# GpSimd takes two steps of the weight preparation in a fused attention and FFN kernel on one core, with the order of the work set anew

## The chip, the cores and the metric

The kernel runs on one core of one Trainium2 chip. The metric is device time in microseconds (us) of one execution. Before the change the median of three runs is 1265.73 us (1262.9 to 1267.84).

## The reference, cut to what matters

Eight batches of eight heads attend over 576 positions with head size 64; only scores within `tau` of the row's maximum count. The heads' outputs, side by side, go through an FFN whose activation is a ratio of polynomials.

```python
scores = scale * (q @ k.T)
thresh = scores.max(-1) - tau
attn = softmax(where(scores >= thresh, scores, -1e9))
x = (attn @ v) as [8*576, 512]
h = x @ w_in                      # 512 -> 2048
g = (a0 + a1*h + a2*h**2 + a3*h**3) / (1 + |b0|*|h| + |b1|*h**2 + 1e-6)
out = g @ w_out                   # 2048 -> 512
```

## The kernel before, in words

**Attention.** The heads of a batch are taken in four pairs; a unit is one block of 128 queries of a pair (`unit_ops`, L767), and the last 64 rows of both heads make a half unit. TensorE forms the scores (L810, for half units L800), VectorE takes their maximum (L818), ScalarE thresholds and exponentiates (L833, L837), and ScalarE and VectorE split the result into a high and a low fp16 part (L347, L859), which DMA transposes on SyncE's queue turn around (L869). For the first batch `f_diag` and `f_tr` (L875, L882, L887) transpose on TensorE instead and `f_avp` (L912) multiplies by V; later `f_av` (L928) does. The result is split again into `x` (L938, L944).

**FFN.** `moe_ops` takes 256 positions and four of the sixteen groups of 128 hidden columns at a time: first layer (L1045), scale (L1054), the rational function on ScalarE and VectorE (L1059 to L1087), split into `g` (L339, L1095), second layer (L1104).

**Weights.** Both weight matrices arrive as 64-bit words, each word the bits of a double. `decode_ops` (L483) turns a tile of 128x512 of them into fp32, for 16 tiles of `w_in` and 16 of `w_out`. `ld` issues the transfer on GpSimd's queue; `f1` (L506, ScalarE) takes the high words; `f2` (L509, ScalarE) scales the low words by 2^-29; `f4` (L513, VectorE) shifts; `f6` (L354, VectorE) adds both. For `w_out`, `f_wh` rounds to the 'wh' part (L341 or L339) and `f_wl` (L593, VectorE) forms the remainder. Each is needed before the first FFN block that uses its group. A wait keeps transfers apart: a tiny GpSimd instruction (L498) reads the third last tile when that was issued within the last 9 us.

**V.** `load_v_ops` (L680) clears two corners of a V tile (L690), loads it (L696, L700) on GpSimd's queue, and takes its maximum (`mx`, L711 or L709). After a batch's fourth maximum `scale_ops` (L427) makes the batch's scale: two VectorE steps (L437, L442), one matmul (`f_all`, L446), more VectorE steps. Four V tiles exist, so a load waits until the attention that used the tile has multiplied by it.

**Order.** Nothing is ordered by the engines at run time. Every step is recorded with `op(engine, duration, key, function, ...)`, and `Plan.order` (L193) lists them: it keeps a clock for each engine, lets the ready step with the lowest key start, and picks the engine of a step that may run on two. `TURN` and `KIND` are tables added to the keys, `EARLY` and `PRICE` weigh ScalarE against VectorE. 'GD' is GpSimd's queue, whose steps before were transfers only. Where the plan sees TensorE idle in its first 400 us, it puts filler matmuls (`f_warm`, L1248) into 0.6 of the gap; the fillers compute nothing that is used.

Of the kernel before, what the change touches and what calls it, by code (L numbers as in the profile page):

```python
# [80 lines left out]
EARLY = {"ACT": 1.6309, "DVE": 3.9296}  # L81
EARLY_END = 714.5248
PRICE = {"ACT": 0.9171, "DVE": 2.3360}

TURN = [
# [22 lines left out]
KIND = [  # L108
# [8 lines left out]
BEGIN = 1.4  # L117
WIRE, LATER = 1.25, 0.3
# [22 lines left out]
class Plan:  # L141
# [3 lines left out]
    LAT = {"PE": 0.27, "ACT": 0.28, "DVE": 0.22, "POOL": 0.16, "DMA": 2.3, "GD": 2.7}  # L145
    OWN = {"PE": 0.0, "ACT": 0.15, "DVE": 0.13, "POOL": 0.1, "DMA": 2.3, "GD": 2.7}
# [15 lines left out]
    def op(self, eng, dur, key, fn, after=(), take=(), drop=(), wire=None):  # L162
        engs = {eng: dur} if isinstance(eng, str) else eng
        o = Op(engs, key, fn, [x for x in after if x is not None], list(take), list(drop))
        o.wire = wire and (wire[0] * WIRE, wire[1] + LATER)
        o.turn, o.kind = self.turn, self.kinds.setdefault(fn.__code__, len(self.kinds))
        turn = TURN[o.turn] / 1000 if o.turn < len(TURN) else 0.0
        o.key += turn
        o.key += KIND[o.kind] / 1000 if o.kind < len(KIND) else 0.0
        o.rank = self.rank + turn  # L170
        self.ops.append(o)
        return o
# [20 lines left out]
    def order(self):  # L193
# [19 lines left out]
        left, wire = len(self.ops), 0.0  # L213
        while left:
# [28 lines left out]
            o.eng, o.dur = e, o.engs[e]  # L243
            for x in o.engs:
# [53 lines left out]
def masked_attention_rational_ffn(  # L298
# [28 lines left out]
    for name, n in [*POOLS.items(), ("q", NQ), ("k", NQ), ("v", NV)]:  # L327
        plan.pool(name, n)
# [962 lines left out]
```

## Time and profile before

| what | value |
|---|---|
| median of the runs, us | 1265.73 |
| profiled execution: time, us | 1266.8 |
| profiled execution: span, first to last instruction, us | 1265.0 |
| TensorE matmul busy | 1226.9 us, 97% |
| VectorE busy | 1188.0 us, 94% |
| ScalarE busy | 1118.3 us, 88% |
| GpSimd busy | 97.8 us, 8% |
| TensorE's mean granted clock, share of full | 0.991 |

The 1.8 us between time and span lie outside the profiled instructions. The busy shares are averages over stages with different limits: weights are prepared in the first 160 us, attention and FFN run side by side until 1140 us, and only FFN is left after it.

### The profile page before, as it was taken

How to read it: one execution, taken by the hardware profiler on the slowest of the kernel's cores; microseconds unless marked ns; L12 is line 12 of the kernel's file. 1: busy time of each engine (PE TensorE's matmuls, PEld its weight loads, DVE VectorE, ACT ScalarE, POOL GpSimd, SP SyncE). 2: the span in 40 equal slices, each digit the busy share in tenths (PEclk: the TensorE clock that was granted, in tenths of full speed). 3: DMA queues.
4: the chain of work that ended last, by engine and by line, in shares of the span. 5: the costliest groups of instructions: out<-in, count | busy, mean ns of one | idle time of the engine just before them, and what ended most of it. 6: DMA issues, size and time to landing. Idle time of an engine off the chain costs nothing. (4 is left out here: it accounts for less than half of the span.)

```text
span 1265.0 us, 25738 instructions
## 1 busy us (share of the span) xinstructions
PE 1226.9 (97%) x9650; PEld 961.6 (76%) x9650; DVE 1188.0 (94%) x1830; ACT 1118.3 (88%) x2185; POOL 97.8 (8%) x217
## 2 busy tenths in 40 slices
PE   8899999999999999999999999999999989999998
PEld 6677777777777777767777777777777767778886
DVE  6999899999999999999999899999999979998787
ACT  7999999999989899988898999899999979895564
POOL 4110000010001100101001100021001100000000
PEclk9999999999999999999999999999999989999999
DMA  6454644675556654665664666667456664542000
GB/s 193 136 167 129 149 81 85 134 151 119 114 95 146 126 110 102 124 121 89 124 116 80 131 125 96 122 120 139 90 112 125 132 109 88 116 88 45 18 17 17
DMA packets 338603, 138.54 MB, mean 110 GB/s; under 512 B 312624, under 2 KB 321712, under 8 KB 338480
## 3 DMA queue, kind: packets, MB, share of 16 engines
q1 hardware_dynamic: 326656, 103.40, 43.9%
q0 software_dynamic: 11072, 32.91, 8.9%
q8 instruction: 76, 1.25, 0.4%
q10 hardware_dynamic: 752, 0.59, 0.2%
q14 instruction: 47, 0.39, 0.1%
HBM read 52.17 MB, written 9.44 MB: 49 GB/s over the span
## 5 line engine op out<-in xcount | busy, mean ns | idle before, releaser
L1104 PE MATMUL banks<-wp,g 128*128 128x512 f32 x1728 | 449.1, 408 | 3.2 <-DVE g L1095 1.7
L1104 PEld LDWEIGHTS banks<-wp,g 128*128 128x128 f32 x1728 | 317.1, 191 | 82.6 <-DVE g L1095 4.4
L1045 PEld LDWEIGHTS <-wi 128*128 128x128 f16 x3456 | 328.8, 98 | 65.3 <-issue 23.3
L1045 PE MATMUL banks<-x,wi 128*128 128x256 f16 x3072 | 360.4, 274 | 3.8 <-ACT t L1054 3.3
L837 ACT ACTIVATE e<-e,cf 128x576 f32<-128x576 f32 x288 | 222.3, 779 | 0.2
L859 DVE SCALAR_TENSOR_TENSOR e<-e,st,hi 128x576 f16<-128x576 f32 x252 | 204.3, 811 | 7.2 <-ACT hi L347 6.5
L833 ACT ACTIVATE e<-banks,st 128x576 f32<-128x576 f32 x288 | 207.2, 739 | 4.2 <-DMA pT<-e 1.9
L347 ACT ACTIVATE hi<-e,st 128x576 f16<-128x576 f32 x225 | 171.0, 770 | 30.2 <-DVE st L848 25.3
L810 PE MATMUL banks<-KK,QQ 64*128 64x64 f32 (+1 forms) x1024 | 175.5, 455 | 7.4 <-ACT e L833 4.5
L818 DVE TENSOR_REDUCE st<-banks 128x2 f32<-128x1152 f32 x128 | 172.3, 1346 | 8.0 <-PE banks L810 7.2
L810 PEld LDWEIGHTS banks<-KK,QQ 64*128 64x128 f32 x1024 | 115.1, 188 | 77.0 <-issue 46.9
L1054 ACT ACTIVATE t<-banks,hsc 128x512 f32<-128x512 f32 (+1 forms) x192 | 106.6, 577 | 26.0 <-PE banks L1045 16.4
L928 PE MATMUL banks<-pT,V 128*64 128x256 f16 (+1 forms) x2520 | 121.7, 250 | 2.6 <-DVE xr L944 2.4
L928 PEld LDWEIGHTS <-V 128*64 128x64 f16 x2520 | 103.7, 111 | 23.3 <-issue 18.8
L1081 DVE SCALAR_TENSOR_TENSOR t<-t,co,t 128x1024 f32<-128x1024 f32 (+1 forms) x73 | 92.2, 1263 | 18.7 <-ACT t L1075 18.6
L1072 ACT ACTIVATE t<-t,co 128x1024 f32<-128x1024 f32 (+1 forms) x73 | 82.9, 1136 | 28.3 <-DVE t L1078 27.0
L1095 DVE TENSOR_TENSOR g<-t,g 128x512 fp32r<-128x512 f32 x144 | 95.2, 683 | 0.8 <-ACT g L339 0.7
L1087 DVE SCALAR_TENSOR_TENSOR t<-t,co,t 128x1024 f32<-128x1024 f32 (+1 forms) x73 | 92.2, 1264 | 0.6
L1065 DVE SCALAR_TENSOR_TENSOR t<-t,co 128x1024 f32<-128x1024 f32 (+1 forms) x73 | 92.2, 1263 | 0.3 <-ACT t L1054 0.3
L1068 DVE SCALAR_TENSOR_TENSOR t<-t,co 128x1024 f32<-128x1024 f32 (+1 forms) x73 | 92.2, 1263 | 0.0
L1078 DVE SCALAR_TENSOR_TENSOR t<-t,co,t 128x1024 f32<-128x1024 f32 (+1 forms) x73 | 92.2, 1263 | 0.0
L1084 DVE SCALAR_TENSOR_TENSOR t<-t,t 128x1024 f32<-128x1024 f32 (+1 forms) x73 | 87.9, 1204 | 0.5
(116 smaller groups left out, 1183.5 us busy)
## 6 DMA issues: line engine op xcount, KB each, us to landing
KK<-in_kT_dram SPq DMA_DIRECT2D x108, 144.0 KB, 3.0
t<-in_w_in_dram POOLq DMA_DIRECT2D x16, 512.0 KB, 4.9
t<-in_w_out_dram POOLq DMA_DIRECT2D x16, 512.0 KB, 4.8
V<-in_v_dram POOLq DMA_DIRECT2D x28, 256.0 KB, 4.4
out_dram<-u POOLq DMA_DIRECT2D x26, 256.0 KB, 3.0
QQ<-in_qT_dram SPq DMA_DIRECT2D x72, 64.0 KB, 2.3
pT<-hi SPq DMA_TRANSPOSE x140, 3.3
pT<-e SPq DMA_TRANSPOSE x140, 3.3
```

Of the source, the lines that this page charges most:

```text
L347: nc.scalar.activation(dst, src, AF.Identity, scale=factor)
L810: mm = nc.tensor.matmul(s[:, d0:d0 + n], QQ[r, t * P:(t + 1) * P], KK[r, k0:k0 + n], **one)
L818: nc.vector.tensor_reduce(box["st"][:, 0:2], box["both"], AX.X, ALU.max, negate=True)
L833: nc.scalar.activation(ev(hh), box["s"][hh], AF.Prelu, scale=SCALE, bias=box["st"][:, 2 + hh:3 + hh], alpha=STEEP)
L837: nc.scalar.activation(e, e, AF.Exp, scale=passes, accum_out=box["st"][:, 4 + hh:5 + hh])
L859: nc.vector.scalar_tensor_tensor(box["lo"][:, c], ev(hh), box["st"][:, 6 + hh:7 + hh], box["hi"][:, c], ALU.mult, ALU.subtract)
L928: nc.tensor.matmul(dst, V[:, c * P + hh * D:c * P + (hh + 1) * D], rhs, start=c == 0 and n == 0, stop=c == NT and n == 2)
L1045: nc.tensor.matmul(d, wi_tile(c, f0 + j, hl), x[:, c, :], start=c == 0 and n == 0, stop=c == NC - 1 and n == 2)
L1054: nc.scalar.activation(box["h3"][:, 2 * k:2 * k + 2, sl], psv[:, :, sl], AF.Identity, scale=hsc[:, b2, g:g + 1])
L1065: nc.vector.scalar_tensor_tensor(box["r"], box["h"], a2, box["h"], ALU.add, ALU.mult)
L1095: nc.vector.tensor_tensor(fr(g[:, 1]), box["r"][:, k * GW:(k + 1) * GW], g[:, 0], ALU.subtract)
L1104: nc.tensor.matmul(acc[tt], fr(g[:, x]), fr(wo[f][y]), start=begins and j == n == 0, stop=ends and j == nb - 1 and n == 2)
```

## The change

The step `f2` goes from ScalarE to GpSimd. The step `f_wl` goes from VectorE to GpSimd. Both are put into the plan's queue 'GD' with the transfers, so that the plan decides where on GpSimd's queue each stands; the tiny waiting instruction L498 goes, and a pool "w" of three takes its place: a weight transfer takes a slot and `f2` gives it back. A matmul of another layout than the one before costs the plan 0.093 us more, and the durations of attention's matmuls are lowered by about two such amounts. The plan expects V's transfers to land later. All order tables are new; only a line of each is shown. Lines of the changed kernel lie 2 to 5 higher in number (L509 is L510, L593 is L595, L446 is L451, L1248 is L1250).

```diff
-EARLY = {"ACT": 1.6309, "DVE": 3.9296}
+EARLY = {"ACT": 1.6376, "DVE": 3.8765}
-PRICE = {"ACT": 0.9171, "DVE": 2.3360}
+PRICE = {"ACT": 0.9166, "DVE": 2.2665}
 TURN = [
-    -22753, -3751, -27085, -7959, -27620, -11402, -9570, -6508, -9214, -7383, -6968, -3656, -3744, -4154, -5879,
+    -22753, -7303, -14653, -13042, -55886, -12787, -11115, 320, -22676, -1808, -1997, -1589, 541, -2218, -1953, 992,
...
+TURNS = 0.093
...
-    LAT = {"PE": 0.27, "ACT": 0.28, "DVE": 0.22, "POOL": 0.16, "DMA": 2.3, "GD": 2.7}
-    OWN = {"PE": 0.0, "ACT": 0.15, "DVE": 0.13, "POOL": 0.1, "DMA": 2.3, "GD": 2.7}
+    LAT = {"PE": 0.27, "ACT": 0.28, "DVE": 0.22, "POOL": 0.16, "DMA": 2.3, "GD": 0.2}
+    OWN = {"PE": 0.0, "ACT": 0.15, "DVE": 0.13, "POOL": 0.1, "DMA": 2.3, "GD": 0.1}
...
+            if e == "PE":
+                o.dur += TURNS if o.mode != mode else 0.0
+                mode = o.mode
...
-            if len(loaded) >= AHEAD and plan.now - loaded[-AHEAD][1] < RECENT:
-                nc.gpsimd.tensor_scalar(cf[0:1, 15:16], loaded[-AHEAD][0][0:1, 0, 1:2].bitcast(F32), 1.0, 1.0, ALU.mult, ALU.mult)
             box["rw"] = load()
-            loaded.append((box["rw"], plan.now))
+            loaded.append(box["rw"])
...
         def f2():
-            nc.scalar.activation(box["rw"][:, :, 0], box["rw"][:, :, 0].bitcast(U32), AF.Copy, scale=2.0 ** -29)
+            nc.gpsimd.tensor_scalar(box["rw"][:, :, 0], box["rw"][:, :, 0].bitcast(U32), 2.0 ** -29, 1.0, ALU.mult, ALU.mult)
...
-        l = op("GD", 2.5, key - 2.0, ld, (), [hold], wire=(1.9, 2.0))
+        wh = Hold("w", 1)
+        l = op("GD", 0.65, key - 2.0, ld, (), [hold, wh], wire=(1.9, 2.3))
...
-        o2 = op("ACT", 0.568, key, f2, [l])
+        o2 = op("GD", 0.87, key, f2, [l], (), [wh])
...
         def f_wl(f=f, box=box):
-            nc.vector.tensor_tensor(fr(wo[f][1]), box["w"], wo[f][0], ALU.subtract)
+            nc.gpsimd.tensor_tensor(fr(wo[f][1]), box["w"], wo[f][0], ALU.subtract)
...
-        wo_done.append(op("DVE", 0.66, key, f_wl, [o], (), [hold]))
+        wo_done.append(op("GD", 1.5, key, f_wl, [o], (), [hold]))
...
-        l = v_loaded[bp] = op(eng, 1.7 if eng == "DMA" else 2.0, max(q, V0 + V1 * pr), ld, (), [vhold], wire=(1.1, 1.5 if eng == "DMA" else 2.5))
+        l = v_loaded[bp] = op(eng, 1.7 if eng == "DMA" else 2.0, max(q, V0 + V1 * pr), ld, (), [vhold], wire=(1.1, 3.0 if eng == "DMA" else 4.5))
...
-        qk = op("PE", 1.36 if full else 1.12, p, f_qk, need, [sh[0]], [kh, qh] * nh)
+        qk = op("PE", 1.175 if full else 0.935, p, f_qk, need, [sh[0]], [kh, qh] * nh, mode=1)
```

The change moves instructions in three places that the prediction speaks of. The first is GpSimd's queue behind the first V loads, where the weights come in; `t` are tiles that hold weights, and `wp` is where the second layer's weights end. Before:

```order
L546 DMA t_68<-in_w_in_dram 128x1024
L546 DMA t_69<-in_w_in_dram 128x1024
L582 DMA t_70<-in_w_out_dram 128x1024
L498 TENSOR_SCALAR cf<-t_68 1x1
L546 DMA t_71<-in_w_in_dram 128x1024
L498 TENSOR_SCALAR cf<-t_69 1x1
L546 DMA t_72<-in_w_in_dram 128x1024
L696 DMA V_157<-in_v_dram 128x4x128
L700 DMA V_157<-in_v_dram 64x64 x2
L546 DMA t_73<-in_w_in_dram 128x1024
```

And now:

```order
L548 DMA t_68<-in_w_in_dram 128x1024
L584 DMA t_69<-in_w_out_dram 128x1024
L548 DMA t_70<-in_w_in_dram 128x1024
L698 DMA V_157<-in_v_dram 128x4x128
L702 DMA V_157<-in_v_dram 64x64 x2
L510 TENSOR_SCALAR t_68<-t_68 128x512
L548 DMA t_71<-in_w_in_dram 128x1024
L510 TENSOR_SCALAR t_69<-t_69 128x512
L548 DMA t_72<-in_w_in_dram 128x1024
L510 TENSOR_SCALAR t_70<-t_70 128x512
L548 DMA t_73<-in_w_in_dram 128x1024
L510 TENSOR_SCALAR t_71<-t_71 128x512
L595 TENSOR_TENSOR wp_1_123<-t_69,wp_0_122 128x512
```

The fourth V load now stands ahead of the fourth weight transfer, and each later transfer stands behind arithmetic on an earlier tile.

The second place is ScalarE's queue in the same stretch, from the second block's exponential on; `u` holds high words, `pT` transposed scores. Before:

```order
L837 ACTIVATE e_78,st_85<-e_78,cf 128x576 x2
L509 ACTIVATE t_68<-t_68 128x512
L509 ACTIVATE t_69<-t_69 128x512
L833 ACTIVATE e_79<-banks,st_86 128x576
L339 COPY pT_82<-banks 128x4x128
L506 ACTIVATE u_76<-t_68 128x512
L339 COPY pT_82<-banks 128x4x128
L339 COPY pT_82<-banks 128x128
L506 ACTIVATE u_74<-t_69 128x512
```

And now:

```order
L507 ACTIVATE u_74<-t_68 128x512
L839 ACTIVATE e_78,st_85<-e_78,cf 128x576 x2
L835 ACTIVATE e_79<-banks,st_86 128x576
L556 ACTIVATE t_68,wm<-t_68 128x512
L344 COPY pT_82<-banks 128x4x128
L835 ACTIVATE e_79<-banks,st_86 128x576
L344 COPY pT_82<-banks 128x4x128
```

The two low-word steps between the exponential and the copies for TensorE's transposes are gone. Over the whole program ScalarE loses all 32 low-word steps and VectorE all 16 remainders; TensorE's fillers go from 81 matmuls to 60, and the number of its changes between scores, attention outputs and the rest from 450 to 449.

The third place is TensorE ahead of a late batch's scale matmul, from the last use of the V tile whose reload that scale waits for. Before, at the last batch (between the rows shown stand 24 first-layer matmuls L1045 and 12 second-layer matmuls L1104):

```order
L928 MATMUL banks<-pT_83,V_156 64x64
...
L1045 MATMUL banks<-x_98,wi 128x256
...
L1104 MATMUL banks<-wp_1_125,g_96 128x512
L810 MATMUL banks<-KK_115,QQ_111 128x64
L810 MATMUL banks<-KK_115,QQ_111 128x512 x2
...
L1104 MATMUL banks<-wp_0_126,g_94 128x512 x2
L1104 MATMUL banks<-wp_1_127,g_94 128x512
L446 MATMUL banks<-u_76,cf 128x128
```

And now, at the last batch but one (between the rows stand 24 L1047, four matmuls of scores, three L1106 and six L1047):

```order
L930 MATMUL banks<-pT_83,V_157 64x64
L812 MATMUL banks<-KK_115,QQ_111 128x64
L812 MATMUL banks<-KK_115,QQ_111 128x512 x2
...
L1047 MATMUL banks<-x_98,wi 128x256
...
L812 MATMUL banks<-KK_114,QQ_110 128x512 x2
...
L1106 MATMUL banks<-wp_1_123,g_95 128x512
...
L1047 MATMUL banks<-x_97,wi 128x256
L451 MATMUL banks<-u_76,cf 128x128
```

At this place the changed order has less work between the two than any batch after the first has in the order before; at the last batch it has more.

## Rows read from the trace of the kernel before

**Rows 1.** The view by stage: the stretch and its length in us, the busy time of PE, PEld, DVE, ACT and POOL with their instructions in brackets, TensorE's granted clock as a share of full, the DMA engines' busy share and GB/s.

```profile
20.00:160.00 140.00, 128.62 (x994) 100.14 (x992) 128.29 (x301) 137.84 (x305) 15.96 (x31) 0.99 0.50 143
160.00:540.00 380.00, 377.07 (x3074) 294.56 (x3074) 375.48 (x546) 358.83 (x695) 27.75 (x62) 1.00 0.58 116
540.00:1040.00 500.00, 483.81 (x3880) 377.54 (x3879) 476.52 (x707) 450.77 (x884) 38.78 (x86) 0.98 0.61 114
...
1140.00:1265.00 125.00, 120.00 (x799) 98.35 (x797) 98.03 (x104) 68.12 (x110) 0.00 (x0) 0.99 0.10 22
```

**Rows 2.** The same view for the fillers (L1248) alone; each filler leaves two matmul records.

```profile
0.00:20.00 20.00, 6.50 (x36) 5.83 (x36) 1.00 0.84 231
20.00:160.00 140.00, 15.00 (x92) 12.76 (x92) 0.99 0.50 143
160.00:360.00 200.00, 4.88 (x34) 4.27 (x34) 1.00 0.57 113
```

**Rows 3.** The waits of TensorE from 20 to 160 us: who waited for whom, us in total, times, longest.

```profile
PE banks L882 <- ACT pT L339: 2.8, 4, 1.1
PE banks L882 <- DVE st L827: 2.3, 1, 2.3
```

**Rows 4.** The view by stage for L509 alone (ScalarE, the low words), 20 to 160 us: busy us and how many.

```profile
20.00:160.00 140.00, 21.07 (x30) 0.99 0.50 143
```

**Rows 5.** VectorE's groups from 20 to 160 us, shapes apart: count | busy us, mean ns | idle before.

```profile
L354 DVE CUSTOM_DVE_ANT_0 t<-t,u 128x1024 uint16<-128x1024 uint16 x31 | 21.2, 688 | 0.9 <-issue 0.3
L513 DVE TENSOR_SCALAR u<-u 128x512 int32<-128x512 int32 x31 | 13.0, 422 | 1.1 <-ACT u L506 1.0
L570 DVE SCALAR_TENSOR_TENSOR wi<-t,sw,wi 128x512 f16<-128x512 f32 x16 | 11.8, 745 | 0.0
L593 DVE TENSOR_TENSOR wp<-t,wp 128x512 fp32r<-128x512 f32 x15 | 10.2, 684 | 0.0
```

**Rows 6.** GpSimd's groups over the whole span, same columns.

```profile
L498 POOL TENSOR_SCALAR cf<-t 1x1 f32<-1x1 f32 x7 | 1.6, 221 | 8.7 <-issue 4.0 <-DMA t<-in_w_in_dram 3.3 <-DMA t<-in_w_out_dram 1.4
masks.py:199 POOL TENSOR_SCALAR_AFFINE_SELECT ident<-ident 128x128 f32<-128x128 f32 x1 | 0.3, 292 | 0.1
L494 POOL TENSOR_SCALAR cf<-KK 128x1 f32<-128x1 f32 x1 | 0.2, 197 | 0.0
```

**Rows 7.** Instructions of VectorE and GpSimd in order of time, 47.5 to 49.6 us: start, duration, engine, line.

```profile
47.78 0.43 DVE L341 CAST wp<-t 128x512 fp32r<-128x512 f32 x1
47.91 0.34 POOL L498 TENSOR_SCALAR cf<-t 1x1 f32<-1x1 f32 x1 [3.96 <-issue]
...
48.85 0.42 DVE L513 TENSOR_SCALAR u<-u 128x512 int32<-128x512 int32 x1
49.01 0.30 POOL L498 TENSOR_SCALAR cf<-t 1x1 f32<-1x1 f32 x1
```

**Rows 8.** The same at 1002 us, and behind it VectorE's group that the stretched instruction belongs to, over the whole span.

```profile
1002.32 0.76 POOL L696 DMA_DIRECT2D V<-in_v_dram  x1
...
1002.57 0.78 DVE L349 TENSOR_SCALAR hi<-e,st 128x576 f16<-128x576 f32 x1
...
L349 DVE TENSOR_SCALAR hi<-e,st 128x576 f16<-128x576 f32 x27 | 14.2, 524 | 0.3
```

**Rows 9.** In order of time, all engines, 1008 to 1021.5 us: the last batch's fourth V load and what waits for it.

```profile
1008.29 0.34 POOL L690 MEMSET V<- 64x64 f32 x2 [4.17 <-PE banks L928]
...
1019.28 0.74 ACT L711 ACTIVATE u<-V 128x640 bf16<-128x640 f32 x1 [4.92 <-DMA V<-in_v_dram]
...
1021.33 0.58 PE L446 MATMUL banks<-u,cf 128*128 128x128 f32 x1 [4.26 <-DVE u L442]
```

**Rows 10.** The same chain of an earlier batch, 434 to 442.6 us.

```profile
434.13 0.34 POOL L690 MEMSET V<- 64x64 f32 x2 [16.33 <-PE banks L928]
...
442.43 0.39 PE L446 MATMUL banks<-u,cf 128*128 128x128 f32 x2
```

**Rows 11.** The view by stage, 1020 to 1028 us.

```profile
1020.00:1028.00 8.00, 6.67 (x27) 4.89 (x28) 7.12 (x19) 6.78 (x14) 0.00 (x0) 0.57 0.75 164
```

**Rows 12.** Pieces of the chain that ended last, where TensorE runs without a gap: start, us, what.

```profile
1080.76 2.62 PE banks L1045 x24
1083.38 1.40 PE banks L1104 x6
1084.78 1.23 PE banks L810 x6
```

**Rows 13.** The waits of the whole span: who waited for whom, us in total, times, longest.

```profile
PE banks L446 <- DVE u L442: 4.9, 2, 4.3
```

**Rows 14.** TensorE in order of time, 540 to 760 us: the first instructions behind its gaps, the gap in brackets.

```profile
557.70 0.40 PE L810 MATMUL banks<-KK,QQ 64*128 64x64 f32 x2 [2.08 <-DMA KK<-in_kT_dram]
...
579.64 4.09 PE L1045 MATMUL banks<-x,wi 128*128 128x256 f16 x36 [1.77 <-ACT t L1054]
691.66 0.66 PE L928 MATMUL banks<-pT,V 128*64 128x64 f16 x30 [2.40 <-DVE xr L944]
741.71 1.35 PE L810 MATMUL banks<-KK,QQ 64*128 64x64 f32 x8 [1.66 <-ACT e L833]
744.52 7.22 PE L1104 MATMUL banks<-wp,g 128*128 128x512 f32 x24 [1.46 <-ACT u L1115]
```

More of the change, by code (lines that the diff above doesn't have):

```diff
@@ L160, in pool, with op @@
         self.pools[name] = [(0.0, i) for i in range(n)]
-    def op(self, eng, dur, key, fn, after=(), take=(), drop=(), wire=None):
+    def op(self, eng, dur, key, fn, after=(), take=(), drop=(), wire=None, mode=0):
         engs = {eng: dur} if isinstance(eng, str) else eng
         o = Op(engs, key, fn, [x for x in after if x is not None], list(take), list(drop))
+        o.mode = mode
         o.wire = wire and (wire[0] * WIRE, wire[1] + LATER)
@@ L212, in order @@
         done, busy = [], dict.fromkeys(engines, 0.0)
-        left, wire = len(self.ops), 0.0
+        left, wire, mode = len(self.ops), 0.0, 0
         while left:
@@ L326, in masked_attention_rational_ffn @@
     op = plan.op
-    for name, n in [*POOLS.items(), ("q", NQ), ("k", NQ), ("v", NV)]:
+    for name, n in [*POOLS.items(), ("q", NQ), ("k", NQ), ("v", NV), ("w", AHEAD)]:
         plan.pool(name, n)
@@ L997, in unit_ops @@
         if plain:
-            av = op("PE", 2.36 if full else 0.76, p + 1.2, f_avp, two["tp"] + [v_loaded[bp], x_first.get(ck)], [bh] + first, [two["pT"], vh_[bp]])
+            av = op("PE", 2.175 if full else 0.575, p + 1.2, f_avp, two["tp"] + [v_loaded[bp], x_first.get(ck)], [bh] + first, [two["pT"], vh_[bp]], mode=2)
             plain_av.setdefault(bp, []).append(av)
         else:
-            av = op("PE", 1.86 if full else 0.69, p + 1.2, f_av, two["tp"] + [v_low(bp), x_first.get(ck)], [bh] + first, [two["pT"], vh_[bp]])
+            av = op("PE", 1.675 if full else 0.505, p + 1.2, f_av, two["tp"] + [v_low(bp), x_first.get(ck)], [bh] + first, [two["pT"], vh_[bp]], mode=2)
         x_first.setdefault(ck, av)
```

50 rows, old and new, of tables (KIND, TURN) are left out of this document.

## The prediction

> **What bounds the kernel now.** I began with the view by stage [rows 1], because the shares of the whole span hide where an engine is short. From 160 to 540 us TensorE is busy 377 of 380 us, and after 1140 us nothing but FFN matmuls is left, 120 of 125 us. So the end of the kernel is set by TensorE: its work, which the change leaves alone, plus the time in which it does none. From 540 to 1040 us it stands for 16.2 us. From 20 to 160 us the reader should see another limit: ScalarE is busy 137.8 of 140 us, VectorE 128.3, TensorE 128.6. And of TensorE's 128.6 us, 15.0 are fillers [rows 2], matmuls that stand where the plan saw nothing to do. Idle and fillers together, TensorE loses 11.4 + 15.0 = 26.4 us in this stage. The third view is who TensorE waits for there [rows 3]: the two longest lines are 2.8 us for ScalarE's copies of transposed scores and 2.3 us for VectorE. The early stage is short of ScalarE, the rest of TensorE.
>
> **The change part by part.**
>
> *Low words leave ScalarE.* 30 of the 32 steps lie in this stage and take 21.1 us of ScalarE [rows 4], 15% of it. All of it lies on the engine that is short, but the end moves only by what TensorE no longer loses: at least 0, at most 26.4 us. Which part? The changed order has 60 fillers where the order before had 81. The 162 records took 26.4 us [rows 2], 0.326 us for a filler, so 21 fewer are 6.8 us of TensorE's time. The remaining waits of 11.4 us were not in the plan before, and nothing in the order says that they will be fewer; I leave them as they are. Early term: -6.8 us, between 0 and -26.4.
>
> *Remainders leave VectorE.* 15 of 16 lie in this stage, 10.2 us [rows 5]. VectorE is not the shorter engine there, having 11.7 us of idle time [rows 1], so this gives nothing by itself. It gives VectorE room: 21.9 us in all.
>
> *Both arrive on GpSimd.* The trace has no GpSimd arithmetic on a tile of this size. The nearest row that reads and writes one is the affine select on 128x128, 292 ns; a column of one element takes 197 ns [rows 6]. That is 0.75 ns for a further column, and for 512 columns an estimate of 0.58 us for one input, and 0.97 us with the slope doubled for two. In sum 32 x 0.58 + 16 x 0.97 = 34 us, which is the low end. The high end is where GpSimd's queue would itself be short: it is busy 16 us of the stage [rows 1], which leaves 124 us, or 2.6 us for each of 48 steps. I take the low end, the affine select being the nearest row. Transfers now queue behind arithmetic, which itself waits for a landing or for another engine's half; with 34 us in 124 the queue is mostly idle, and I cost this at nothing. The cover is that idle time. It is gone at 2.6 us a step, when weights come late and ScalarE's gain is lost too.
>
> *GpSimd beside VectorE.* Here the trace warns. Seven GpSimd instructions on a single element average 221 ns [rows 6]. Two of them took 0.34 and 0.30 us beside a cast and a shift of VectorE, which leaves 0.18 us for each of the other five, and both times GpSimd ended just after VectorE's instruction did, 48.25 against 48.21 us and 49.31 against 49.27 [rows 7]. VectorE can wait too: beside the issue of a V load one instruction took 0.78 us against 0.52 us for its group, a third of the 0.76 us of the issue [rows 8]. So the engines get in each other's way. If VectorE loses a quarter of GpSimd's 34 us, that is 8.6 us, and the room of 21.9 us hides it. Bounds: 0, and three quarters of 34 us, 26 us, which is above the room. I take 8.6 us, since the measured third was the worst of the rows I saw.
>
> The Trainium skill, page "SBUF — State Buffer", section "Who interferes with whom", is sterner: GpSimd and VectorE share one pair of ports, and a VectorE instruction with two SBUF inputs, or in a two-port mode, blocks a GpSimd instruction that reads SBUF, or is blocked by it, for the whole of it. The row of the cast agrees for the wait of GpSimd; no row here shows a two-input instruction beside a reading GpSimd one. By this rule the hidden 8.6 us would be nearer the upper bound, and the sum would be that of the first rival.
>
> *Changes of matmul layout* go from 450 to 449: nothing.
>
> *V's loads.* The longest of TensorE's gaps is 4.26 us at 1017 us, and behind it the clock: from 1020 to 1028 us the granted clock was 0.57, so part of that stretch ran at the lower of the two levels, 1.2 GHz, right after the gap, and cost 8 x 0.43 = 3.4 us [rows 9, 11]. Its chain begins when the tile's last reader is done; from the corners' clearing to the scale's matmul it took 13.0 us, most of it landing. In an earlier batch the same chain took 8.3 us and TensorE did not wait [rows 10]. TensorE had 24 + 18 + 4 matmuls to do meanwhile, 2.6 + 4.2 + 1.2 = 8.0 us, with a step of scores taken as its whole piece [rows 12]. In the changed order the last batch has more, some 12 us, but the one before only 2 x 1.23 + 30/24 x 2.62 + 0.70 = 6.4 us. So the old gap goes, -4.3 - 3.4, and a new one opens: 8.3 - 6.4 = 1.9 us with a fast landing, 6.6 us with a slow one. I take 1.9, as only two of twelve such matmuls waited before, the other one 0.6 us [rows 13], and half the old clock loss, 1.7 us. Together -4.1 us, between -7.7 and +2.3.
>
> *The other gaps* from 540 to 760 us sum to 9.4 us in these rows and wait for K, for ScalarE and for VectorE [rows 14]. A new order deals them anew; I cost that at nothing, give or take 6 us.
>
> **Sum.** -6.8 - 4.1 = -10.9 us on the profiled execution of 1266.8 us, 1255.9 us. That execution stands 1.1 us above the median of runs spread over 5 us; I keep 1256 us.
>
> **The rivals.**
>
> *GpSimd holds VectorE up (slower).* The weight stage becomes VectorE's. For it: [rows 7, 8], and that groups which work between SBUF tiles fill most of VectorE's stage, L354, L513 and L570 alone 46 us [rows 5]. Against it: most GpSimd transfers before left VectorE's times alone. Price: VectorE's 128.3 - 10.2 + 26 = 144 us of work in a stage of 140 that also had 11.7 us of idle time from waits. If two thirds of those waits stay, the stage takes 152 us, +12. With the V term, 1266.8 + 12 - 4 = 1275 us. It decides from a loss of 21.9 us on, 0.46 us for each of the 48 steps. The Trainium skill's rule speaks for this one.
>
> *The gain is spent on the way (no change).* VectorE is busy 375 of 380 us in the stage behind [rows 1]. What TensorE wins early it may wait out later, when VectorE cannot deliver faster, and new gaps fall where old ones went. Then only a third of the 10.9 us remains: 1263 us.
>
> *More goes than I count (faster).* ScalarE lost 21 us and VectorE some too; if the 11.4 us of unfilled waits shrink by half and the gaps of [rows 14] shrink by half with V's later planning, that is another 5.7 + 4.7 us: 1245 us.
>
> *Weights come late.* One queue now holds transfers, low words and remainders in order, and a remainder that waits for its rounded half stops the transfers behind it. For the time of one landing on each of the four weight groups, some 2 us each, the early gain is gone: 1264 us. I count it with the second rival.
>
> **How the numbers follow.** Forecast 0.42, GpSimd holding VectorE up 0.19, gain spent or weights late 0.25, more than counted 0.14. A measurement of this kernel can tell about 0.5% from no change, that is 6.3 us: faster means below 1259.4 us, slower above 1272.1. The forecast's own range is 1249 to 1264, four fifths of it faster: 0.34 + 0.14 and 0.02 of the second rival make 0.50. Of the slower rival, 0.16 lies above 1272 and 0.02 of the others: 0.18. The rest is 0.32. The range reaches to the first rival's time and short of the fast one's lower half: 1243 to 1276 us.
>
> **What would show it.** Right: from 20 to 160 us ScalarE no longer full, TensorE's idle and filler time down by about 7 us, VectorE's instructions near their means of [rows 5], the remainder and low-word steps on GpSimd near 0.6 and 1.0 us, no gap of 4 us at the last scale's matmul and one of some 2 us at the scale before. Wrong: L354 or L570 stretched by half a us in many instances, VectorE full in that stage, and TensorE's gaps in it as long as before or longer; or the early gap smaller and the sum of gaps after 540 us larger by as much.

## The result, and the profile of the changed kernel

| | before | after |
|---|---|---|
| median of the runs beside each other, us | 1263.93 | 1273.05 |
| ratio, 95% interval | | 1.0061 [1.0036, 1.0087] |
| profiled execution, its span, us | 1266.8, 1265.0 | 1273.72, 1272.0 |

The change made the kernel 0.61% slower, 7.7 us of 1264; the forecast was 10.9 us faster. The ratio is taken from undisturbed executions alone, so it is not the quotient of the medians. The diagonal step, L875 before, is L877 in the changed kernel; in kernels of the experiments that add lines, numbers are higher by a few more. The view by stage, columns as in [rows 1], with the first 20 us of before ahead, which [rows 1] does not have:

```profile
0.00:20.00 20.00, 17.70 (x96) 13.62 (x97) 10.58 (x35) 11.95 (x26) 13.11 (x34) 1.00 0.84 231
```

```profile
0.00:20.00 20.00, 15.05 (x100) 12.36 (x100) 10.77 (x35) 12.49 (x28) 14.72 (x35) 1.00 0.84 242
20.00:160.00 140.00, 123.51 (x938) 94.19 (x934) 126.11 (x268) 123.36 (x277) 57.74 (x69) 0.98 0.42 134
160.00:540.00 380.00, 369.26 (x2999) 288.13 (x2999) 374.52 (x543) 350.96 (x687) 29.45 (x59) 1.00 0.59 115
540.00:1040.00 500.00, 488.02 (x3897) 377.15 (x3894) 479.29 (x694) 450.99 (x888) 41.12 (x92) 0.99 0.59 116
```

And the fillers alone, as in [rows 2]:

```profile
0.00:20.00 20.00, 6.17 (x36) 5.60 (x36) 1.00 0.84 242
20.00:160.00 140.00, 8.25 (x52) 6.63 (x52) 0.98 0.42 134
160.00:360.00 200.00, 4.66 (x32) 4.04 (x32) 0.99 0.60 114
```

Read them as TensorE's idle time plus fillers. From 20 to 160 us ScalarE is relieved (137.8 us busy in [rows 1], 123.4 now) and fillers fall from 15.0 to 8.25 us, as forecast. But idle time grows from 11.4 to 16.5 us, so that only 1.6 us of the 6.8 remain. Before 20 us 2.3 us are lost (2.3 idle + 6.5 before; 4.95 + 6.2 now), from 160 to 540 us 7.6 us (2.9 + 4.9; 10.7 + 4.7), and from 540 to 1040 us 4.2 us are won (16.2; 12.0). Sum +4.1 of the 7.0 us between the spans. The other 2.9 us lie, all but 0.3, in TensorE's busy time; what makes them is left open.

The next view shows what happened early: GpSimd's two new groups over the whole span, then VectorE's groups from 20 to 160 us (count | busy us, mean ns | idle before).

```profile
L510 POOL TENSOR_SCALAR t<-t 128x512 int32<-128x512 uint32 x32 | 26.2, 817 | 18.8 <-DMA t<-in_w_in_dram 11.5 <-DMA t<-in_w_out_dram 5.6
L595 POOL TENSOR_TENSOR wp<-t,wp 128x512 fp32r<-128x512 f32 x16 | 22.8, 1422 | 41.6 <-DVE wp L346 23.0 <-ACT wp L344 14.8 <-DVE hsc L1214 3.3
...
L359 DVE CUSTOM_DVE_ANT_0 t<-t,u 128x1024 uint16<-128x1024 uint16 x29 | 20.4, 706 | 1.2
L514 DVE TENSOR_SCALAR u<-u 128x512 int32<-128x512 int32 x29 | 13.4, 467 | 3.3 <-ACT u L507 3.3
L572 DVE SCALAR_TENSOR_TENSOR wi<-t,sw,wi 128x512 f16<-128x512 f32 x16 | 13.4, 850 | 0.0
L877 DVE TENSOR_SCALAR u<-ident,st 128x128 f32<-128x128 f32 x31 | 10.7, 368 | 0.3
L829 DVE TENSOR_SCALAR st<-st,cf 128x2 f32<-128x2 f32 x11 | 5.0, 452 | 0.1
```

Two of these groups in before:

```profile
L875 DVE TENSOR_SCALAR u<-ident,st 128x128 f32<-128x128 f32 x32 | 8.7, 279 | 0.1
L827 DVE TENSOR_SCALAR st<-st,cf 128x2 f32<-128x2 f32 x12 | 2.7, 224 | 0.1
```

GpSimd takes 0.82 and 1.42 us a step, 49 us in all, where I had 34. VectorE's shift rose from 422 to 467 ns and its two-input step L572 from 745 to 850 ([rows 5]); the threshold's mean doubled. Summed over VectorE's instructions of the first 185 us, each against the median of its kind in before, the stretch is 15.5 us, nearly all of it in some 30 instructions that stood beside GpSimd arithmetic. I call this sum "the stretch" below; it is good to about 0.5 us, by the choice of the kinds. In order of time, 47 us into the changed kernel (start, duration, engine, line):

```profile
47.06 1.55 DVE L877 TENSOR_SCALAR u<-ident,st 128x128 f32<-128x128 f32 x2
...
47.23 1.30 POOL L595 TENSOR_TENSOR wp<-t,wp 128x512 fp32r<-128x512 f32 x1 [1.72 <-DVE wp L346]
...
48.53 0.41 DVE L514 TENSOR_SCALAR u<-u 128x512 int32<-128x512 int32 x1
```

The reader is to see that the second of two diagonals, a step of 0.28 us, ends only behind the remainder, at 48.61 against 48.53 us. The waits it leads to, TensorE's from 20 to 160 us and then VectorE's own:

```profile
PE banks L884 <- DVE u L877: 4.2, 5, 1.3
PE banks L451 <- ACT e L835: 3.6, 2, 3.0
PE banks L914 <- ACT pT L344: 2.6, 3, 1.0
...
DVE st L850 <- ACT st L844: 4.1, 2, 3.2
DVE u L514 <- ACT u L507: 3.3, 6, 1.1
DVE pT L346 <- PE banks L889: 2.1, 1, 2.1
DVE sc L455 <- PE banks L451: 1.5, 3, 1.0
```

The Trainium skill, page "SBUF — State Buffer", section "Who interferes with whom", has this as an exclusive lock: of a VectorE instruction in a two-port mode, or with two SBUF inputs, and a GpSimd instruction that reads SBUF, the one issued first keeps the shared ports for its whole length and the other waits. The trace agrees where the remainder is first: the diagonal starts 0.03 us behind it and ends 0.08 us behind its end.

### The profile page after: what moved, and what is told of

The parts are those of the page before. It is cut to its first block, busy times and chain, and to the rows that moved or that the text cites. A ratio compares the mean times of both kernels' runs of the same rounds, so it can differ in the third digit from the quotient of the medians.

```text
span 1272.0 us, 25610 instructions
## 1 busy us (share of the span) xinstructions
PE 1222.2 (96%) x9608; PEld 953.2 (75%) x9608; DVE 1193.6 (94%) x1797; ACT 1104.6 (87%) x2171; POOL 145.2 (11%) x258
## 5 line engine op out<-in xcount | busy, mean ns | idle before, releaser
L1106 PE MATMUL banks<-wp,g 128*128 128x512 f32 x1728 | 449.7, 406 | 3.3 <-DVE g L1097 1.9
L1047 PEld LDWEIGHTS <-wi 128*128 128x128 f16 x3456 | 329.5, 99 | 76.8 <-issue 33.2
L1047 PE MATMUL banks<-x,wi 128*128 128x256 f16 x3072 | 366.1, 275 | 9.6 <-ACT t L1056 8.5
L1106 PEld LDWEIGHTS banks<-wp,g 128*128 128x128 f32 x1728 | 313.7, 189 | 81.0 <-issue 4.1
L835 ACT ACTIVATE e<-banks,st 128x576 f32<-128x576 f32 x288 | 204.5, 736 | 6.4 <-DMA pT<-e 3.4
L812 PE MATMUL banks<-KK,QQ 64*128 64x512 f32 (+1 forms) x1024 | 173.2, 451 | 7.7 <-ACT e L835 3.5
```

The source lines that it names most:

```text
L812: mm = nc.tensor.matmul(s[:, d0:d0 + n], QQ[r, t * P:(t + 1) * P], KK[r, k0:k0 + n], **one)
L835: nc.scalar.activation(ev(hh), box["s"][hh], AF.Prelu, scale=SCALE, bias=box["st"][:, 2 + hh:3 + hh], alpha=STEEP)
L1047: nc.tensor.matmul(d, wi_tile(c, f0 + j, hl), x[:, c, :], start=c == 0 and n == 0, stop=c == NC - 1 and n == 2)
L1106: nc.tensor.matmul(acc[tt], fr(g[:, x]), fr(wo[f][y]), start=begins and j == n == 0, stop=ends and j == nb - 1 and n == 2)
```

## Experiments

Theories, as the expectations name them. **A**: GpSimd's steps hold small VectorE steps that lie on the softmax chain, and their lateness is the price. **B**: the new order is worse by itself. **D**: GpSimd's queue is late. **E**: the relief is given back later whatever GpSimd does. **F**: the sum of VectorE's time counts, wherever it is spent. Ratios are to before, with 95% intervals. The runs stood on several chips, on which the kernel before took 1263.9 to 1267.3 us, so kernels are best compared by their ratios.

### The steps or the order?

Old order, both steps on GpSimd, then one of them alone:

```diff
-            nc.scalar.activation(box["rw"][:, :, 0], box["rw"][:, :, 0].bitcast(U32), AF.Copy, scale=2.0 ** -29)
+            nc.gpsimd.tensor_scalar(box["rw"][:, :, 0], box["rw"][:, :, 0].bitcast(U32), 2.0 ** -29, 1.0, ALU.mult, ALU.mult)
...
-            nc.vector.tensor_tensor(fr(wo[f][1]), box["w"], wo[f][0], ALU.subtract)
+            nc.gpsimd.tensor_tensor(fr(wo[f][1]), box["w"], wo[f][0], ALU.subtract)
```

Both: 

> The kernel before in its own order, with its low words and remainders both issued on GpSimd in place of ScalarE and VectorE, nothing else changed. Theory B (the steps are good, the order is bad): ScalarE is relieved of 21 us and the time falls to 1252 to 1260. Theory A: what ScalarE gains is lost to held VectorE steps, 1262 to 1272.

Low words alone: 

> The kernel before in its own order, with the low words alone issued on GpSimd. With both steps there it was 1.0046 of before. Theory A: the shorter step holds VectorE less and ScalarE is relieved of 21 us: 1258 to 1266. If the relief is worth nothing in this order: 1266 to 1272.

Remainders alone: 

> The kernel before in its own order, with the remainders alone issued on GpSimd. VectorE loses 11 us of work of its own, which it did not lack, and is held some 7 us beside it. Theory A: slower than before, 1267 to 1274. If work taken from VectorE is worth more than the holding costs: 1260 to 1266.

Measured: 1273.9 us, 1.0046 [1.0015, 1.0076]; 1270.4 us, 1.0045 [1.0016, 1.0075]; and 1271.9 us, 1.0048 [1.0017, 1.0079]; with a stretch of 17.2, 8.1 and 11.6 us. Each step by itself makes the old kernel slower, although each takes work from ScalarE or VectorE. For both steps B is out: the old order is no faster with them than the new one. The time of the low words is that of their second expectation, but it does not show by itself that the relief is worth nothing, since the 8.1 us of stretch stand in it. The remainders alone came out as theory A had them.

The new order, with steps given back to the old engines (the same lines, the other way round):

Remainders back: 

> The changed kernel in its own order, with the remainders alone given back to VectorE (0.68 us each there, 16 of them). Theory A: VectorE pays 10.9 us of work again but is no longer held by the long GpSimd step; it has room in that stage, so a little faster than the changed kernel, 1266 to 1271. Theory B: no faster, 1272 to 1276, as the order stays and VectorE has more to do.

Both back: 

> The changed kernel in its own order, with low words given back to ScalarE and remainders to VectorE, so that only the order (and the plan's rules) differ from the kernel before. Theory A: no arithmetic on GpSimd, so no stretched VectorE step and under 1 us of waits for the diagonals; ScalarE has its 21 us again in an order that did not plan for them: 1264 to 1271. Theory B: the order costs the whole difference, 1271 to 1277.

Low words back: 

> The changed kernel in its own order, with the low words alone given back to ScalarE; the remainders stay on GpSimd. Theory A: the remainder is the step that holds VectorE for long (1.4 us against 0.8), so most of the loss stays, and ScalarE pays 21 us again: 1270 to 1276. Theory B: as with both given back.

Once more: 

> The changed kernel with the remainders alone given back to VectorE, once more, for its trace and beside the run with the small steps in other forms: 1268 to 1272, as at first; TensorE's waits for the diagonals between 1.8 us (both short) and 6.9 us (both on GpSimd).

Measured: remainders back 1270.8 us, 1.0028 [1.0007, 1.0049] and, again, 1270.0 us, 1.0024 [0.9995, 1.0052], as theory A and the repeat's expectation had it, with waits for the diagonals of 4.9 us; both back 1282.9 us, 1.0136 [1.0100, 1.0171]; low words back 1284.5 us, 1.0141 [1.0106, 1.0176]. The last two lie above every range that I gave, by some 6 us and more. With both back the stretch is 0.4 us, and TensorE waits 4.1 us for diagonals all the same, where theory A gave under 1 us; so such waits are no sure sign of a hold. With ScalarE's 21 us returned the new order is slower than either kernel. An order made for one load of the engines does not bear another. So neither the order nor the steps can be judged alone in this kernel.

### How much GpSimd reads

Remainders on 32 of 512 columns, then both steps:

```diff
-            nc.gpsimd.tensor_tensor(fr(wo[f][1]), box["w"], wo[f][0], ALU.subtract)
+            nc.gpsimd.tensor_tensor(fr(wo[f][1])[:, 0:32], box["w"][:, 0:32], wo[f][0][:, 0:32], ALU.subtract)
...
-                nc.tensor.matmul(acc[tt], fr(g[:, x]), fr(wo[f][y]), start=begins and j == n == 0,
+                nc.tensor.matmul(acc[tt], fr(g[:, x]), fr(wo[f][0]), start=begins and j == n == 0,
```

> The changed kernel, with GpSimd's remainder step on 32 of 512 columns and the remainder matmuls reading the rounded half instead, so the remainders are left out of the result. All of the order stays. Theory A (GpSimd's two-input step holds up small VectorE steps of the softmax chain): the 16 steps shrink from 1.42 to about 0.3 us, the diagonal steps of VectorE come back from 368 to about 300 ns, TensorE's waits for them from 20 to 160 us fall from 6.9 us to about 2, and the time falls by 4 to 9 us, to 1264 to 1269. Theory B (the new order is worse by itself): the waits behind 160 us stay and the time is that of the changed kernel, 1271 to 1275.

Both short (also `[:, 0:32, 0]` in the low words' step, and `t, t, ALU.bitwise_or` for the sum with them): 

> The changed kernel, with both GpSimd steps on 32 of 512 columns; the weights' sum takes no low word in and the remainder matmuls read the rounded half, so low words and remainders are left out of the result. Order, ScalarE's and VectorE's steps stay in number and size. Theory A (the reads of GpSimd beside VectorE eat the relief): with them gone the change gives something at last, 1257 to 1263, and TensorE's waits for the diagonals are under 1.5 us. Theory E (the relief is given back behind 160 us whatever GpSimd does): as with the remainder alone short, 1264 to 1267.

Each remainder twice: 

> The changed kernel, with each remainder step of GpSimd issued twice, same operands: GpSimd gets 16 more steps of some 1.4 us, 23 us in all. Theory A: twice as many VectorE steps are caught, so the loss that the remainder causes doubles: 4 to 9 us slower than the changed kernel, 1277 to 1282. Theory B: GpSimd is busy 58 of 140 us and has room for 23 more, so within 2 us of the changed kernel, 1271 to 1275.

Two fills, `nc.gpsimd.memset(wo[f][1], 0.0)`, ahead of each remainder: 

> The changed kernel, with two fills of the remainder's tile with zero put ahead of each remainder step on GpSimd: GpSimd gets longer as when each step was issued twice, but the added instructions read nothing. Theory A as first put (it is reads of two tiles by GpSimd that hold VectorE): the added time holds nothing, TensorE's waits for the diagonal steps stay near 6.9 us, and the time is that of the changed kernel, 1270 to 1277. Theory A2 (any GpSimd instruction on SBUF holds VectorE) and theory D (GpSimd's queue is late: weights and transfers behind the longer steps) both give the time of the doubled steps, 1283 to 1289; they differ in the trace: under A2 VectorE's steps are stretched beside the fills and TensorE waits for the diagonals, under D it waits for weights.

Each remainder in four pieces of 128 columns: 

> The changed kernel, with each remainder step of GpSimd cut into four of 128 columns, same work. If a VectorE step is held until the end of one GpSimd instruction (theory A), the longest hold of a diagonal falls from 1.35 to some 0.65 us, TensorE's waits for them from 6.9 to about 4 us, and the time to 1267 to 1271. If it is the reading itself that is shared (theory A3), the loss follows the columns and stays: 1272 to 1277.

| kernel | median, us | ratio | stretch, us | TensorE's waits for diagonals, to 180 us |
|---|---|---|---|---|
| both short | 1262.4 | 0.9971 [0.9942, 1.0000] | 1.4 | 1.8 |
| remainder short | 1265.6 | 0.9989 [0.9966, 1.0012] | 5.7 | 2.9 |
| changed | 1273.1 | 1.0061 [1.0036, 1.0087] | 15.5 | 6.9 |
| remainder in four | 1274.6 | 1.0072 [1.0043, 1.0101] | 15.5 | 6.2 |
| fills added | 1275.3 | 1.0069 [1.0044, 1.0093] | 20.2 | 7.5 |
| remainder twice | 1286.8 | 1.0152 [1.0120, 1.0185] | 27.6 | 12.7 |

The remainders, GpSimd's fills and the four pieces, one row of each kernel with its mean in ns:

```profile
L596 POOL TENSOR_TENSOR wp<-t,wp 128x512 fp32r<-128x512 f32 x14 | 19.7, 1406 | 1.1
```

```profile
L595 POOL MEMSET wp<- 128x512 f32 x16 | 9.3, 580 | 0.6
```

```profile
L597 POOL TENSOR_TENSOR wp<-t,wp 128x128 fp32r<-128x128 f32 x64 | 36.4, 597 | 37.8 <-DVE wp L346 21.2 <-ACT wp L344 11.4 <-DVE hsc L1216 3.3
```

The 32 fills add 18.4 us to GpSimd and cost 1 us, within the interval; the second remainders add 16 x 1.4 = 22 us and cost 11.5 us, 5 us above what theory A gave. So it is not GpSimd's queue (D is out), and fills hold little. Four pieces take 2.4 us instead of 1.4, but stretch VectorE by the same 15.5 us: the loss did not follow GpSimd's time. My hope that cutting frees the small steps failed where pieces follow each other without a gap, so the run does not tell A from A3, whose time came true. Here the second of two diagonals of 0.28 us ends 0.1 us behind the third piece:

```profile
54.67 1.81 DVE L879 TENSOR_SCALAR u<-ident,st 128x128 f32<-128x128 f32 x2
55.08 1.72 POOL L597 TENSOR_TENSOR wp<-t,wp 128x128 fp32r<-128x128 f32 x4
```

With both short, the view by stage, and its fillers from 0 to 360 us:

```profile
0.00:20.00 20.00, 15.40 (x98) 12.57 (x100) 10.57 (x35) 12.17 (x27) 13.70 (x35) 1.00 0.85 226
20.00:160.00 140.00, 129.09 (x996) 99.09 (x995) 121.22 (x277) 128.95 (x290) 30.74 (x69) 0.98 0.46 141
160.00:540.00 380.00, 373.57 (x3026) 291.78 (x3024) 376.37 (x547) 354.28 (x694) 28.64 (x64) 1.00 0.61 117
540.00:1040.00 500.00, 487.54 (x3945) 377.95 (x3944) 481.65 (x705) 453.07 (x890) 38.51 (x86) 0.99 0.60 116
...
0.00:20.00 20.00, 6.34 (x36) 5.67 (x36) 1.00 0.85 226
20.00:160.00 140.00, 8.24 (x52) 6.63 (x52) 0.98 0.46 141
160.00:360.00 200.00, 4.66 (x32) 4.04 (x32) 0.99 0.61 117
```

From 20 to 160 us TensorE now loses 10.9 + 8.24 = 19.1 us, 7.2 less than before. The forecast had 6.8. The rest of the order costs 2.1 us before 20 us and 3.3 us from 160 to 540 us, and wins 3.7 us from 540 to 1040 us. Short steps also take away that VectorE's sum and the remainder matmuls wait for GpSimd's results. That is not what slows the changed kernel: up to 180 us its trace shows no wait of VectorE or TensorE for a low word or a remainder. The sum without low words is no shorter, 0.69 us as before.

### Which VectorE steps?

Diagonals on ScalarE, `nc.scalar.activation(box["dg"][...], ident, AF.Copy, scale=...)`: 

> The changed kernel, with the 36 diagonal steps of the softmax chain (identity times the reciprocal, 128x128) issued on ScalarE instead of VectorE. Theory A: they are no longer held, TensorE's waits for them of 6.9 us go to about 1, ScalarE gains some 36 x 0.3 = 11 us of which most has room in the early stage: 3 to 7 us faster than the changed kernel, 1266 to 1270. Theory B: nothing gained, 1272 to 1277.

Other forms on VectorE (ident2 is a copy of the identity with every second word empty):

```diff
-                nc.vector.tensor_scalar(d, m, SCALE, taue, ALU.mult, ALU.add)
+                for x in range(h1 - h0):
+                    nc.vector.tensor_scalar(d[:, x:x + 1], m[:, x:x + 1], SCALE, taue, ALU.mult, ALU.add)
...
-            nc.vector.tensor_scalar(box["dg"][:, hh * P:(hh + 1) * P], ident, box["st"][:, 6 + hh:7 + hh], None, ALU.mult)
+            nc.vector.tensor_scalar(box["dg"][:, hh * P:(hh + 1) * P], ident2, box["st"][:, 6 + hh:7 + hh], None, ALU.mult)
```

> The changed kernel, with the small VectorE steps of the softmax chain written in other forms: the identity of the diagonal steps is read from a copy with every second word empty, and thresholds and sums before the reciprocal are formed column by column (128x1, the form that was not stretched beside GpSimd in the changed kernel) instead of 128x2. Theory A (latency of these steps on the chain): they are no longer held, TensorE's waits for the diagonals fall from 6.9 to under 2.5 us and the time to 1263 to 1268. Theory F (the sum of VectorE's stretched work): the long two-input steps are held as before, 1270 to 1275. If the strided diagonal is held all the same, the trace shows steps of over 0.6 us beside the remainder, and the time is that of the changed kernel.

And with remainders back: 

> As the run with the small steps in other forms, and the remainders given back to VectorE; the low words stay on GpSimd. Without the forms the remainders' return gave 1.0028 of before. Theory A: the low words' share of the holding goes too, 1262 to 1267, so no slower than before at the least. Theory F: 1268 to 1272.

Diagonals that also sum (the same, but `ident, ..., 0.0, ALU.mult, ALU.add, accum_out=junk1`): 

> The changed kernel, with thresholds and sums formed column by column as in the run with other forms, and the 36 diagonal steps of VectorE in the form that also writes the sum of its output (into an unused column). The Trainium skill, page SBUF - State Buffer, says of that form that it does not enter the two-port mode; if so no diagonal is over 0.6 us. Theory A (latency of the small steps): TensorE's waits for the diagonals fall from 6.4 to under 2.5 us, the time to 1263 to 1268. Theory F (the sum of VectorE's stretched work, the long two-input steps above all): waits fall, the time stays, 1270 to 1275. If the diagonals are held all the same, the time is 1272 to 1277 and this is left open.

And with remainders back: 

> The same with the remainders back on VectorE, the low words on GpSimd. Without the forms that was 1.0024 and 1.0028 of before. Theory A: 1262 to 1267. Theory F: 1268 to 1272.

Measured: diagonals on ScalarE 1277.5 us, 1.0090 [1.0055, 1.0124], no gain; they take 36 x 0.39 us there, and TensorE waits 6.3 us for them all the same. Other forms 1273.5 us, 1.0053 [1.0030, 1.0075]; the thresholds were freed (none stretched), the strided diagonals were not, up to 1.35 us. With remainders back 1273.5 us, 1.0051 [1.0031, 1.0071]. Summing diagonals 1276.3 us, 1.0093 [1.0057, 1.0129], with remainders back 1275.8 us, 1.0086 [1.0052, 1.0121]. Both runs with remainders back came out above the ranges of A and of F, and the summing kernel above F's by 1 us. The rows of the summing kernel, 20 to 160 us and then in order of time:

```profile
L880 DVE TENSOR_SCALAR_CACHE_REDUCE u<-ident,st 128x128 f32<-128x128 f32 x31 | 10.6, 341 | 1.0
L831 DVE TENSOR_SCALAR st<-st,cf 128x1 f32<-128x1 f32 x23 | 3.9, 205 | 0.1
...
47.52 1.30 POOL L596 TENSOR_TENSOR wp<-t,wp 128x512 fp32r<-128x512 f32 x1 [1.71 <-DVE wp L346]
47.82 0.35 DVE L880 TENSOR_SCALAR_CACHE_REDUCE u<-ident,st 128x128 f32<-128x128 f32 x1
48.09 0.08 DVE L880 DVE_READ_ACCUMULATOR u<-ident,st 128x1 f32 x1
48.17 0.93 DVE L515 TENSOR_SCALAR u<-u 128x512 int32<-128x512 int32 x1
```

All 36 diagonals took 0.33 to 0.35 us, also in the middle of a remainder, as here. And the kernel was no faster. This is where theory A fell: here the hold passes to the next instruction in VectorE's queue, the shift, 0.93 us instead of 0.42, and TensorE still waits 4.7 us for diagonals, since those come late out of the queue. The stretch was 10.2 us, and the forms cost VectorE some 8 us of their own: 36 diagonals of 0.42 us instead of 0.28, and two columns in place of one step of two for thresholds and sums.

### VectorE's time by itself

Both short, and one line more in the shift of a weight piece:

```diff
             nc.vector.tensor_single_scalar(t, t, 3, ALU.logical_shift_left)
+            nc.vector.tensor_single_scalar(t, t, 0, ALU.logical_shift_left)
```

> As the run with both GpSimd steps on 32 columns (low words and remainders left out of the result), and each of VectorE's 32 shifts of a weight piece is issued a second time, by nought: 32 x 0.42 = 13.5 us more for VectorE, about the 14.1 us by which its steps were stretched in the changed kernel over that run, and nothing more for GpSimd. Theory F (VectorE's time in the early stage is what counts, its idle time being no room): 9 to 14 us slower than with both short, 1271 to 1277, as slow as the changed kernel. Theory A (the small steps of the chain): these are not held, so 1262 to 1267. If VectorE's idle time of the stage is room, as the prediction had it: 1261 to 1264.

Measured: 1272.1 us, 1.0060 [1.0037, 1.0083], with a stretch of 1.1 us. The view by stage, its fillers, and TensorE's waits for diagonals to 180 us:

```profile
20.00:160.00 140.00, 123.63 (x926) 94.03 (x923) 125.88 (x296) 122.77 (x274) 27.49 (x67) 0.96 0.44 135
...
20.00:160.00 140.00, 8.25 (x52) 6.63 (x52) 0.96 0.44 135
...
PE banks L885 <- DVE u L878: 4.2, 5, 1.7
```

GpSimd holds nothing here, yet the kernel is as slow as the changed one, and its early stage is the same: TensorE 123.6 and 123.5 us, VectorE 125.9 and 126.1, ScalarE 122.8 and 123.4. TensorE waits 4.2 us for diagonals that nothing holds. So 32 x 0.425 = 13.6 us of VectorE's time cost 0.89% or 11.3 us, 0.83 us for each, with an interval of 0.5 to 1.2. By that rate the changed kernel's stretch over both short, 14.1 us, makes 11.7 us; measured are 0.90%, 11.4 us (with a 95% interval of some 5 us to either side, from the two ratios'). The doubled remainder's 26.2 us make 21.7; measured 22.9. F fits there, with added time that stood in one place only, at the shift.

It does not fit everywhere. With remainders back VectorE has 16 x 0.68 = 10.9 us of work and 6.8 us of stretch, 16.3 us over both short, by the rate 13.5 us and 1.0078; measured were 1.0024 and 1.0028, some 6 us less. In the old order the remainders alone leave VectorE 11.6 - 10.9 = 0.7 us more, yet cost 0.48%, 6.1 us (2 to 10); there TensorE's waits for diagonals rise from 0.7 to 3.8 us, as A would have it. With the diagonals on ScalarE VectorE has 10 us less of work and some 3 us less of stretch, and the kernel is no faster: ScalarE has 14 us more. And with the low words back on ScalarE the stretch is only 7 us, but the kernel is 10 us slower than the changed one. So ScalarE's time seems to count as well, though no run adds to it alone. F is thus a rule that fits some runs and misses others by 6 us and more; what lies beyond it is left open.

## Why the prediction was wrong

- **GpSimd beside VectorE** is the step that failed. It took 8.6 us of loss and wrote "the room of 21.9 us hides it". The loss was 15.5 us, inside its bounds of 0 to 26 us and below the room, and yet it was not hidden: the changed kernel is 11.4 us slower than with both short. VectorE was busy 126 of 140 us and idle for 14, but most of that is waits for its partners: for ScalarE (4.1 us for L844's results, 3.3 us for L507's) and for TensorE (2.1 and 1.5 us). That time added between such waits moves the whole chain is my reading of it; that added time is not hidden, the run with more shifts shows without any hold by GpSimd.
- The first rival, GpSimd holding VectorE up, came in its direction and near its 1275 us. Its point of decision, 21.9 us or 0.46 us a step, was wrong with the same error: it had decided at 15.5 us, 0.32 us a step. The sign that I had set for it, L354 or L570 longer by half a us in many instances, did not show: these two (now L359 and L572) average 18 and 105 ns more. The hold fell on few instructions, half of it on tensor_scalar steps of 128x2 and 128x128. The second rival, gain spent on the way, is part of it: 160 to 540 us lost 7.6 us, 3.3 of them with both steps short too.
- **GpSimd's steps** took 49 us where I had 34. From the affine select I had 0.97 us for two inputs; the shortest of them took 1.28 us. The queue's time by itself cost nothing: 18.4 us of fills in it did not show.
- **Early term**, -6.8 us: right once nothing is held, -7.2 us, nearly all of it in fillers as forecast; -1.6 us in the changed kernel.
- **V term**, -4.1 us: the stage from 540 to 1040 us came out 4.2 us better. The 4.3 us gap is gone. The new gap of 1.9 us that I expected at the last batch but one did not open; no scale matmul waits behind 540 us. That 4.2 agrees with 4.1 is partly luck: the forecast netted -7.7 against +3.6 us, and what came is the old gap alone. The 3.4 us of lost clock behind it is TensorE's busy time and not in the 4.2; the granted clock of the stage rose only from 0.98 to 0.99.
- **Other gaps**, 0 give or take 6 us: +2.3 us before 20 us and +7.6 us from 160 to 540 us in the changed kernel, +2.1 and +3.3 with both short. So even with next to no hold the change was worth 0.29%, 3.7 us, with an interval from 0 to 7.3, and not 10.9.

No version that computes everything beat the kernel before; the nearest was the low words alone on GpSimd in the new order, 1.0024 and 1.0028.

## What to carry to other kernels

Idle time of an engine is room only if it lies where the added time falls: look at what ends it, and where it is waits for other engines, do not count it as cover: here each us added to VectorE cost 0.83 us, give or take 0.35. Before giving GpSimd arithmetic on SBUF tiles, count VectorE's instructions that it will stand beside, and take the hold as VectorE's work, since freeing one instruction can hand it to the next. Where an order is set for one load of the engines, compare a moved step in both orders, as neither gives the step's worth by itself.

## What the hardware showed that was not expected

- The hold depends on the instruction's form more than its size: a tensor_scalar of 128x2 took up to 1.36 us, while 128x1 and the reciprocal of 128x2 beside the same steps were not stretched. Reading with a stride did not free a diagonal; summing the output did, at 341 + 82 ns against 280. The Trainium skill, page "SBUF — State Buffer", section "Who interferes with whom", names the summing form as the tensor_scalar that does not enter the two-port modes; the trace agrees.
- The same section of the Trainium skill's page "SBUF — State Buffer" has it that two-input VectorE instructions are held only by a GpSimd instruction that reads. The trace agrees: of ten two-input VectorE instructions that overlapped a fill, eight kept within 0.03 us of their usual times, and the two longer ones stood beside a low-word step or a remainder too. Fills cost nothing that can be measured here, though the stretch rose by 4.7 us with them, 3.2 us of it beside fills.
- GpSimd took 0.70 us (median, 0.63 least) for 512 columns of one input, 1.30 us for two, and 0.46 us for two inputs of 128 columns.
